# The second gate half asked for from the ScalarE queue, a slightly later x tile 1, and a fixed place for gelu on ScalarE, in a fused state-space and gated feed-forward kernel

## Chip, cores and metric

The kernel runs on one core of one Trainium2 chip. The metric is the device time of one execution in microseconds (us). The profile of an execution counts its "span" from the first recorded instruction; it is about 1.5 us shorter than the timed run. All runs in this text are in the fast state, except one run of d_before (188.62 us), which is marked slow. Ratios are the mean time of one kernel's fast runs over the mean of the other's fast runs of the same rounds, so they are not quite the ratios of the medians quoted beside them.

## The reference

The input x is 2048 rows of 512 columns in bf16. It is normalised row by row, and two branches read the result: a diagonal complex state-space scan, and a gated feed-forward layer of 1376 hidden columns. The output is their sum with x.

```python
xn = _layernorm(x)                                     # rows of 512
# branch A: h[t] = Lam_bar * h[t-1] + xn[t] @ B_bar.T ; y = 2 Re(h @ C.T) + xn * Dskip
# branch B:
ff = (gelu(xn @ w_gate) * (xn @ w_up)) @ w_down        # 512 -> 1376 -> 512
return x + y + ff
```

## The kernel before

x is cut into 16 tiles of 128 rows, four tiles to a block. TensorE (PE) multiplies, ScalarE (ACT) and VectorE (DVE) empty the PSUM banks and do the rest. The order of TensorE and of SyncE (SP, which issues most DMA) is the order of the program text. The order of ScalarE and VectorE is found by a list scheduler in Python, which works with estimated durations. `order_behind(a, b)` tells it to keep `a` behind `b` on the same engine.

The start of the kernel, with cuts marked:

```python
V(lambda e: e.memset(WRM.ap, 0.0), 150, [], [WRM], "wrm")             # zeros for the warm-up matmuls
half = V(lambda e: e.memset(HALF.ap, 0.5), D_TINY, [], [HALF], "half")
GATE["table"] = ACT(lambda e: e.activation(SCR.ap, HALF.ap[:, 0:1], ACTF.Gelu_apprx_tanh), 100, [HALF], [SCR], "gelu0")
# ... cut ...
ld_x0(0)                                                # x tile 0, 128 KB, SyncE queue
S.order_behind(ld_x0(1, "scalar"), GATE["table"])       # x tile 1, ScalarE queue
ld_wg0(0, "sync")                                       # first gate half: weight rows 0 to 255, 192 KB
ld_wg0(1, "sync")                                       # second gate half: rows 256 to 511
S.order_behind(ld_x0(2, "scalar"), GATE["table"])       # x tile 2
ld_w(WU, WUc, ins["B_w_up"], 0)                         # up weights, 384 KB
ld_x0(3)
# ... cut: the rest of the weights ...
nwarm = 7                                               # matmuls of zeros, before any data is there
# ... cut ...
fill(2)                                                 # two more small ones
cent_T(0, tb, "AA")                                     # transposes of centred tile 0, ScalarE copies them out
cent_T(1, [wb])
for r in range(2): GT_mm(0, r, ub[0, r], [0], (0, 1))   # first gate half, 4 matmuls in all
for r in range(2): GT_mm(0, r, ub[0, r], [0], (2, 3))   # second gate half, 4 matmuls
fill(4)                                                 # four fillers
# ... cut: tile 1's gate group (8), four groups of up weights (16), tile 2's transposes among them ...
```

Later, in the B stage, eight products of x and B for each block go through PSUM, ScalarE copies them out ("B copy"), and the feed-forward part of the next block follows with gelu:

```python
# BU(b): 8 groups of 4 matmuls, each followed by
ACT(lambda e, ...: e.activation(SSc[k3][s][c].ap, PS[bank][:, :], ACTF.Copy), d_act(512), [BANK[bank]], [SSc[k3][s][c]], "evBu")
# GU(b): for each 128 hidden columns
GATE["last_gelu"] = ACT(lambda e, ...: e.activation(GG[kk].ap[0:m, :], PS[bg][0:m, :], ACTF.Gelu_apprx_tanh), ..., "gelu", after=GATE["before_gelu"])
ACT(lambda e, ...: e.activation(UPB[kk].ap[0:m, :], PS[bu][0:m, :], ACTF.Copy), ..., "evU")
```

The kernel uses eight PSUM banks in turn and makes TensorE wait for a bank's copy before it writes the bank again (in x1_late below, 0.5 us for one copy).

Of the kernel before, what the change touches and what calls it, by code (L numbers as in the profile page):

```python
# [10 lines left out]
ACTF = mybir.ActivationFunctionType  # L11
# [350 lines left out]
def d_pe(n_list):  # L362
    return sum(n / 2.4 + 2.5 for n in n_list)
def d_dve_tt2x(n): return 100.0 + 0.52 * n
# [4 lines left out]
def d_act(n, ptr=0): return 190.0 + 0.833 * n + 90.0 * ptr  # L369
# [3 lines left out]
def build(nc, ins, out):  # L373
    with ExitStack() as es:
        E = es.enter_context
        S = Sched(nc, es)
# [3 lines left out]
        PS = [E(nc.psum_tensor("PS%d" % i, [128, 512], F32)) for i in range(8)]  # L380
# [45 lines left out]
        WRM = A.alloc("WRM", [128], BF16)  # L426
# [40 lines left out]
        SSc = [[[A.sub(SSs[k][s], "SS%d_%d_%d" % (k, s, c), c) for c in range(2)] for s in range(KP)] for k in range(3)]  # L467
# [3 lines left out]
        V = lambda fn, dur, r, w, tag="", after=(): S.op("vector", fn, dur, r, w, tag, after)  # L471
        ACT = lambda fn, dur, r, w, tag="", after=(): S.op("scalar", fn, dur, r, w, tag, after)
        POOL = lambda fn, dur, r, w, tag="", after=(): S.op("gpsimd", fn, dur, r, w, tag, after)
        PE = lambda fn, dur, r, w, tag="": S.op("tensor", fn, dur, r, w, tag)

        V(lambda e: e.memset(WRM.ap, 0.0), 150, [], [WRM], "wrm")
        GATE = {"before_gelu": [], "nh": 0}
        SCR = A.alloc("SCR", [1], F32)
        half = V(lambda e: e.memset(HALF.ap, 0.5), D_TINY, [], [HALF], "half")
        GATE["table"] = ACT(lambda e: e.activation(SCR.ap, HALF.ap[:, 0:1], ACTF.Gelu_apprx_tanh), 100, [HALF], [SCR], "gelu0")  # L480
        POOL(lambda e: e.iota(IOT.ap, [[1, 128]], base=0, channel_multiplier=-1), 300, [], [IOT], "iota")
        GATE["ident"] = V(lambda e: e.tensor_scalar(IDN.ap, IOT.ap, 0.0, None, ALU.is_equal), d_dve_ts4x(128), [IOT], [IDN], "ident")
# [9 lines left out]
        def ld_w(W, Wc, src, ci, queue="sync", after=()):  # L492
            f0, f1 = FCH[ci]
            return S.dma(lambda e: e.dma_start(W.ap[:, :, f0:f1], src[:, f0:f1].rearrange("(k p) f -> p k f", p=128)),
                         512 * (f1 - f0) * 2, writes=[Wc[ci]], tag="ld_w", queue=queue, after=after)

        def ld_x0(j, queue="sync", after=()):
            return S.dma(lambda e, j=j: e.dma_start(X[j].ap, x2[128 * j:128 * (j + 1), :]), 128 * 1024, writes=[X[j]], tag="ld_x0", queue=queue, after=after)  # L498
        WG0h = [Buf("WG0h%d" % n, "sbx", n / 2, (n + 1) / 2) for n in range(2)]

        def ld_wg0(n, queue, after=()):
            return S.dma(lambda e: e.dma_start(WG.ap[:, 2 * n:2 * n + 2, 0:384],  # L502
                                        ins["B_w_gate"][256 * n:256 * (n + 1), 0:384].rearrange("(k p) f -> p k f", p=128)),
                  192 * 1024, writes=[WG0h[n]], tag="ld_w", queue=queue, after=after)
        ld_x0(0)
        S.order_behind(ld_x0(1, "scalar"), GATE["table"])
        ld_wg0(0, "sync")
        ld_wg0(1, "sync")
        S.order_behind(ld_x0(2, "scalar"), GATE["table"])
        ld_w(WU, WUc, ins["B_w_up"], 0)  # L510
        ld_x0(3)
        for ci in (1, 2):
# [44 lines left out]
        def next_bank():  # L557
            b_ = rstate["n"] % 8
            rstate["n"] += 1
            return b_  # L560
# [165 lines left out]
        def BU(b):  # L726
            k3 = b % 3
            for c, s in ([(c, s) for c in range(2) for s in range(KP)] if b == 0 else [(c, s) for s in range(KP) for c in range(2)]):
                bank = next_bank()

                def f(e, bank=bank, c=c, s=s, b=b):
                    ins_ = None
                    for dk in range(KD):
                        ins_ = e.matmul(PS[bank][:, :], BBT[c][dk].ap[:, 128 * s:128 * (s + 1)], XNT[b].ap[:, dk, :],  # L734
                                        start=(dk == 0), stop=(dk == KD - 1))
                    return ins_
                PE(f, d_pe([512] * 4), [BBT[c][dk] for dk in range(KD)] + XTr(b), [BANK[bank]], "Bu%d" % b)
                ACT(lambda e, bank=bank, k3=k3, s=s, c=c: e.activation(SSc[k3][s][c].ap, PS[bank][:, :], ACTF.Copy),  # L738
                    d_act(512), [BANK[bank]], [SSc[k3][s][c]], "evBu")

        def span_of(buf, s0, s1):
# [70 lines left out]
        def GU(b, fts=None):  # L812
            k2 = b % 2
            fts = list(range(KF) if fts is None else fts)
            banks = {}

            def mm(ft, W, Wc, bank, c0, c1, rd):
                m = FROWS[ft]

                def f(e):  # L820
                    ins_ = None
                    for dk in range(KD):
                        ins_ = e.matmul(PS[bank][0:m, c0:c1], W.ap[:, dk, 128 * ft:128 * ft + m], XNT[b].ap[:, dk, c0:c1],  # L823
                                        start=(dk == 0), stop=(dk == KD - 1))
                    return ins_
                PE(f, d_pe([c1 - c0] * 4), [Wc[wchunk(ft)]] + rd, [BANK[bank]], "GU%d" % b)

            for ft in fts:
                m = FROWS[ft]
                if m < 128:  # L830
                    GU_rest(b)
                    continue
                banks[ft] = (next_bank(), next_bank())
                bg, bu = banks[ft]
                kk = (KF * b + ft) % 3
                for (W, Wc, bank) in zip((WG, WU), (WGc, WUc), banks[ft]):
                    mm(ft, W, Wc, bank, 0, 512, XTr(b))
                GATE["last_gelu"] = ACT(lambda e, bg=bg, kk=kk, m=m: e.activation(  # L838
                    GG[kk].ap[0:m, :], PS[bg][0:m, :], ACTF.Gelu_apprx_tanh),
                    d_act(512), [BANK[bg]], [GG[kk]], "gelu", after=GATE["before_gelu"])  # L840
                ACT(lambda e, bu=bu, kk=kk, m=m: e.activation(UPB[kk].ap[0:m, :], PS[bu][0:m, :], ACTF.Copy),  # L841
                    d_act(512), [BANK[bu]], [UPB[kk]], "evU")
                V(lambda e, kk=kk, m=m, ft=ft, k2=k2: e.tensor_tensor(  # L843
                    HTt[k2][ft].ap[0:m, :], GG[kk].ap[0:m, :], UPB[kk].ap[0:m, :], ALU.mult),
                  d_dve_tt2x(512), [GG[kk], UPB[kk]], [HTt[k2][ft]], "hmul")
# [144 lines left out]
        TR(1)  # L990
        SKIP(0)
        GU(0, [7, 8, 9, 10])
        GATE["before_gelu"] = [tables_act([GATE["last_gelu"]])]
        SKIP(1)
        BU(0)
        CHAIN(0, 2)
        H0_T()
        BU(1)
        coefs()
        CHAIN(1)  # L1000
# [3 lines left out]
        late_loads()  # L1004
        scale_C()
        GU(1, [0, 1, 2, 10, 3, 4, 5, 6, 7, 8, 9])
        BU(2)
        CHAIN(2)
        DN(0, True)
        LN(3); SKIP(3)  # L1010
        GU(2, [0, 1, 2, 10, 3, 4, 5, 6, 7]); TR(3); GU(2, [8, 9])
        BU(3)
        CHAIN(3)
# [9 lines left out]
def bass_parallel_sum__ssm_conv_s5__geglu_ffn__prompt_kernel(  # L1023
    nc: bass.Bass,
    A_x: bass.AP,
    A_Lambda_re: bass.AP,
    A_Lambda_im: bass.AP,
    A_B_re: bass.AP,
    A_B_im: bass.AP,
    A_C_re: bass.AP,  # L1030
    A_C_im: bass.AP,
    A_log_dt: bass.AP,
    A_Dskip: bass.AP,
    B_x: bass.AP,
    B_w_gate: bass.AP,
    B_w_up: bass.AP,
    B_w_down: bass.AP,
    out: bass.AP,
):
    ins = {  # L1040
        "A_x": A_x, "A_Lambda_re": A_Lambda_re, "A_Lambda_im": A_Lambda_im,
        "A_B_re": A_B_re, "A_B_im": A_B_im, "A_C_re": A_C_re, "A_C_im": A_C_im,
        "A_log_dt": A_log_dt, "A_Dskip": A_Dskip,
        "B_w_gate": B_w_gate, "B_w_up": B_w_up, "B_w_down": B_w_down,
    }
    build(nc, ins, out)
# [28 lines left out]
```

## Time and profile before

| kernel before | |
|---|---|
| timed, three runs at first | 178.21 us median (178.1 to 178.65) |
| timed, six runs when the change was measured | 178.3 us median (178.1 to 178.65) |
| span of the profile | 176.8 us |
| first gate matmul | 5.40 us |
| start of TensorE's unbroken run to the end | 5.98 us |

From the page of the profile: the span, the busy time of the engines (us, share of the span, instructions; PEld is TensorE's weight load), and the shares of the chain that ended last.

```profile
span 176.8 us, 2507 instructions
PE 173.0 (98%) x888; PEld 84.2 (48%) x888; DVE 160.9 (91%) x283; ACT 89.3 (51%) x169; POOL 10.1 (6%) x25
PE 95%; DMA 2%; SPq 0%; DVE 0%; issue 0%
```

The chain is followed back from the last instruction to whatever released each step. In order of time (start, length, what; L698 are the gate and up matmuls of block 0, L920 the fillers, L863 the last products), from its first DMA on:

```profile
1.66 4.27 DMA arena<-in_B_w_gate_dram
5.93 0.05 issue
5.98 0.50 PE PS L698 x4
6.48 0.22 PE PS L920 x4
6.71 0.99 PE PS L698 x12
...
141.37 32.91 PE PS L863 x171
```

The kernel starts on the second gate half, which lands 4.27 us after it is asked for; from there to the end there is nothing but TensorE. The list of waits of the weight loads (us in total, times, longest) has the same wait:

```profile
PEld PS L698 <- DMA arena<-in_B_w_gate_dram: 0.3, 1, 0.3
```

The timeline of TensorE's matmuls in that stretch (start, us from first start to last end, engine, line, shapes, count):

```profile
4.44 0.86 PE L673 MATMUL PS<-arena 128*128 128x128 bf16 x8
5.40 1.08 PE L698 MATMUL PS<-arena 128*128 128x192 bf16 x8
6.32 0.39 PE L920 MATMUL PS<-arena 128*128 128x128 bf16 x4
6.54 1.15 PE L698 MATMUL PS<-arena 128*128 128x192 bf16 x12
7.53 0.39 PE L673 MATMUL PS<-arena 128*128 128x128 bf16 x4
```

From the first gate matmul (5.40) to tile 2's transposes (7.53) are 2.13 us. The work in it is 20 matmuls of 192 columns, which in this trace step by 82.5 ns when TensorE is undisturbed, and 4 fillers that step by 56 ns: 20 x 0.0825 + 4 x 0.056 = 1.87 us. The rest, 0.26 us, is the wait. This stretch, "gate to tile 2", is the ruler.

### The profile page before, as it was taken

To read this page: it belongs to the slowest core of one execution; us is meant where nothing else is said; L and a number is where in the kernel's file an instruction comes from. 1 tells how busy PE (TensorE), PEld (TensorE's weight loads), DVE (VectorE), ACT (ScalarE), POOL (GpSimd) and SP (SyncE) were. 2 spreads that over 40 slices of the span, in tenths; PEclk is the share of its full clock that TensorE was granted. 3 is DMA by queue.
4 is the path that set the end of the run, shared out by engine and by line. 5 is a ranking of instruction groups with operands and counts; after the bars stand their busy time and mean duration, and the time that the engine had idled before them with its cause. 6 is when DMAs were issued, how large, how long until landed. Compare 5 with 4: busy or idle time off the path is not lost.

```text
span 176.8 us, 2507 instructions
## 1 busy us (share of the span) xinstructions
PE 173.0 (98%) x888; PEld 84.2 (48%) x888; DVE 160.9 (91%) x283; ACT 89.3 (51%) x169; POOL 10.1 (6%) x25
## 2 busy tenths in 40 slices
PE   7999999999999999999999999999999999999994
PEld 2854464444544444444644444444454444444453
DVE  5978999998999979979999999899999999999911
ACT  4475578999676898003676593000757680000000
POOL 3212040220000000300000000000000000000000
DMA  5997989675799000011034000100001000000321
GB/s 166 306 317 167 194 193 164 62 150 118 171 255 307 6 0 0 0 61 59 4 61 88 2 0 0 33 30 30 30 0 30 4 0 0 0 0 19 104 77 43
DMA packets 33396, 14.36 MB, mean 81 GB/s; under 512 B 23688, under 2 KB 33384, under 8 KB 33384
## 3 DMA queue, kind: packets, MB, share of 16 engines
q1 hardware_dynamic: 33072, 13.94, 34.7%
q10 hardware_dynamic: 312, 0.27, 0.4%
q8 instruction: 7, 0.11, 0.3%
q14 instruction: 5, 0.04, 0.1%
HBM read 6.46 MB, written 2.10 MB: 48 GB/s over the span
## 4 chain that ended last, share of the span: by engine, by line
PE 95%; DMA 2%; SPq 0%; DVE 0%; issue 0%
PE PS L863 37%; PE PS L823 32%; PE PS L734 16%; PE PS L698 7%; PE PS L797 3%; DMA arena<-in_B_w_gate_dram 2%; PE PS L673 0%; SPq L502 0%; SPq L498 0%; DVE arena L881 0%; PE PS L920 0%
## 5 line engine op out<-in xcount | busy, mean ns | idle before, releaser
L863 PE MATMUL PS<-arena 128*128 128x512 bf16 (+3 forms) x323 | 66.2, 366 | 0.0
L823 PE MATMUL PS<-arena 128*128 128x512 bf16 x264 | 58.1, 379 | 0.0
L863 PEld LDWEIGHTS PS<-arena 128*128 128x128 bf16 (+1 forms) x323 | 30.8, 98 | 35.2
L823 PEld LDWEIGHTS PS<-arena 128*128 128x128 bf16 x264 | 25.8, 98 | 30.4
L838 ACT ACTIVATE arena<-PS 128x512 bf16<-128x512 f32 x33 | 19.8, 600 | 37.6 <-PE PS L823 33.0
L767 DVE TENSOR_TENSOR_SCAN arena<-arena 128x512 bf16<-128x512 f32 x32 | 38.6, 1253 | 0.0
L734 PE MATMUL PS<-arena 128*128 128x512 bf16 x128 | 28.1, 379 | 0.0
L841 ACT ACTIVATE arena<-PS 128x512 bf16<-128x512 f32 x33 | 19.8, 599 | 4.9 <-PE PS L823 4.9
L734 PEld LDWEIGHTS PS<-arena 128*128 128x128 bf16 x128 | 12.5, 98 | 14.9 <-issue 0.2
L855 ACT ACTIVATE PS<-arena 128x512 f32<-128x512 bf16 (+2 forms) x17 | 9.4, 580 | 17.6 <-DVE arena L881 17.1
L738 ACT ACTIVATE arena<-PS 128x512 bf16<-128x512 f32 x32 | 17.4, 604 | 1.1 <-PE PS L734 1.1
L881 DVE TENSOR_TENSOR arena<-PS,arena 128x512 bf16<-128x512 f32 (+2 forms) x17 | 11.0, 654 | 7.3 <-PE PS L863 7.1
L843 DVE TENSOR_TENSOR arena<-arena 128x512 bf16<-128x512 bf16 x33 | 12.9, 415 | 1.0 <-ACT arena L841 0.9
L698 PE MATMUL PS<-arena 128*128 128x192 bf16 (+2 forms) x80 | 13.0, 315 | 0.2
L624 DVE BATCH_NORM_STATS2 arena<-arena 128x6 f32<-128x512 bf16 x16 | 10.2, 682 | 0.8 <-DMA arena<-in_A_x_dram 0.8
L756 DVE TENSOR_TENSOR arena<-arena 128x4096 bf16<-128x4096 bf16 (+1 forms) x5 | 9.2, 1860 | 0.4 <-ACT arena L620 0.4
L698 PEld LDWEIGHTS PS<-arena 128*128 128x128 bf16 x80 | 7.2, 98 | 5.0 <-DMA arena<-in_B_w_gate_dram 0.3
L754 DVE TENSOR_TENSOR arena<-arena 128x4096 bf16<-128x4096 bf16 (+1 forms) x5 | 9.2, 1859 | 0.0
L780 DVE TENSOR_TENSOR arena<-arena 128x4096 bf16<-128x4096 bf16 x4 | 9.1, 2284 | 0.0
L779 DVE TENSOR_TENSOR arena<-arena 128x4096 bf16<-128x4096 bf16 x4 | 9.1, 2283 | 0.0
L707 ACT ACTIVATE arena<-PS,arena 128x192 bf16<-128x192 f32 (+1 forms) x16 | 6.6, 448 | 3.0 <-PE PS L698 2.0
L710 DVE SCALAR_TENSOR_TENSOR arena<-PS,arena 128x192 bf16<-128x192 f32 (+1 forms) x16 | 6.6, 447 | 1.5 <-ACT arena L707 1.3
(84 smaller groups left out, 110.1 us busy)
## 6 DMA issues: line engine op xcount, KB each, us to landing
out_dram<-arena SPq DMA_DIRECT2D x15, 128.0 KB, 1.7
arena<-in_A_x_dram SPq DMA_DIRECT2D x3, 512.0 KB, 5.2
arena<-in_B_w_down_dram SPq DMA_DIRECT2D x1, 1280.0 KB, 7.3
arena<-in_B_w_gate_dram SPq DMA_DIRECT2D x2, 256.0 KB, 5.3
arena<-in_B_w_up_dram SPq DMA_DIRECT2D x2, 256.0 KB, 5.5
arena<-in_B_w_gate_dram SPq DMA_DIRECT2D x1, 480.0 KB, 5.8
arena<-in_B_w_up_dram SPq DMA_DIRECT2D x1, 480.0 KB, 5.9
arena<-arena SPq DMA_TRANSPOSE x25, 2.5
```

The source lines that it names most:

```text
L624: return (V(lambda e: e.bn_stats(ST[tt].ap, X[tt].ap), d_dve_1x(512), [X[tt]], [ST[tt]], "bnst"), V(lambda e: e.bn_aggr(MVt[b][j].ap, ST[t ...
L698: ins_ = e.matmul(dst, XCd(j, k), WGU[:, us[0]:us[-1] + 1, k, f0:f1], start=(k == 0), stop=(k == KD - 1))
L734: ins_ = e.matmul(PS[bank][:, :], BBT[c][dk].ap[:, 128 * s:128 * (s + 1)], XNT[b].ap[:, dk, :], start=(dk == 0), stop=(dk == KD - 1))
L738: ACT(lambda e, bank=bank, k3=k3, s=s, c=c: e.activation(SSc[k3][s][c].ap, PS[bank][:, :], ACTF.Copy), d_act(512), [BANK[bank]], [SSc[k3][ ...
L767: V(lambda e, g=g, rb=rb, init=init: e.tensor_tensor_scan(g.ap, rb, g.ap, init, ALU.mult, ALU.add), d_dve_scan(512), [g, PA[RRr]] + ([CARc ...
L823: ins_ = e.matmul(PS[bank][0:m, c0:c1], W.ap[:, dk, 128 * ft:128 * ft + m], XNT[b].ap[:, dk, c0:c1], start=(dk == 0), stop=(dk == KD - 1))
L838: GATE["last_gelu"] = ACT(lambda e, bg=bg, kk=kk, m=m: e.activation(GG[kk].ap[0:m, :], PS[bg][0:m, :], ACTF.Gelu_apprx_tanh), d_act(512), ...
L841: ACT(lambda e, bu=bu, kk=kk, m=m: e.activation(UPB[kk].ap[0:m, :], PS[bu][0:m, :], ACTF.Copy), d_act(512), [BANK[bu]], [UPB[kk]], "evU")
L843: V(lambda e, kk=kk, m=m, ft=ft, k2=k2: e.tensor_tensor(HTt[k2][ft].ap[0:m, :], GG[kk].ap[0:m, :], UPB[kk].ap[0:m, :], ALU.mult), d_dve_tt ...
L855: ACT(lambda e: e.activation(PS[bank][:, c0:c1], X[tt].ap[:, c0:c1], ACTF.Copy), d_act(c1 - c0), [X[tt]], [BANK[bank]], "seed")
L863: ins_ = e.matmul(PS[bank][:, c0:c1], l_[:, 128 * j:128 * (j + 1)], r_[:, c0:c1], start=False, stop=last and n == len(ops) - 1, skip_group ...
L881: V(lambda e: e.tensor_tensor(OUTB[ko].ap[:, c0:c1], PS[bank][:, c0:c1], XD[tt].ap[:, c0:c1], ALU.add), d_dve_1x(c1 - c0), [BANK[bank], XD ...
```

## The change

The intent is to have the second gate half there when TensorE wants it: it goes second in the ScalarE queue, where x tile 2 was; tile 2 goes third in SyncE's. Tile 1 is asked for a little later (it waits for the second memset), and gelu is tied behind the last B copy.

```diff
-        V(lambda e: e.memset(WRM.ap, 0.0), 150, [], [WRM], "wrm")
         half = V(lambda e: e.memset(HALF.ap, 0.5), D_TINY, [], [HALF], "half")
+        wrm = S.order_behind(V(lambda e: e.memset(WRM.ap, 0.0), 150, [], [WRM], "wrm"), half)
...
         ld_x0(0)
-        S.order_behind(ld_x0(1, "scalar"), GATE["table"])
+        S.order_behind(ld_x0(1, "scalar", [wrm]), GATE["table"])
         ld_wg0(0, "sync")
-        ld_wg0(1, "sync")
-        S.order_behind(ld_x0(2, "scalar"), GATE["table"])
+        S.order_behind(ld_wg0(1, "scalar", [wrm]), GATE["table"])
+        ld_x0(2)
...
-                ACT(lambda e, bank=bank, ...: e.activation(SSc[k3][s][c].ap, PS[bank][:, :], ACTF.Copy),
+                GATE["evBu"] = ACT(lambda e, bank=bank, ...: e.activation(SSc[k3][s][c].ap, PS[bank][:, :], ACTF.Copy),
...
                     d_act(512), [BANK[bg]], [GG[kk]], "gelu", after=GATE["before_gelu"])
+                S.order_behind(GATE["last_gelu"], GATE.pop("evBu", None))
```

More of the change, by code (lines that the diff above doesn't have):

```diff
@@ L737, in BU @@
                 PE(f, d_pe([512] * 4), [BBT[c][dk] for dk in range(KD)] + XTr(b), [BANK[bank]], "Bu%d" % b)
-                ACT(lambda e, bank=bank, k3=k3, s=s, c=c: e.activation(SSc[k3][s][c].ap, PS[bank][:, :], ACTF.Copy),
+                GATE["evBu"] = ACT(lambda e, bank=bank, k3=k3, s=s, c=c: e.activation(SSc[k3][s][c].ap, PS[bank][:, :], ACTF.Copy),
                     d_act(512), [BANK[bank]], [SSc[k3][s][c]], "evBu")
```

## The prediction

> **What bounds the kernel.** TensorE. In the chain of waits it holds 95% of the 176.8 us span, and from 5.98 to 174.29 us the chain is TensorE pieces alone, back to back. VectorE is busy 91%, ScalarE 51% (engine table), and the list of waits shows TensorE waiting for neither in the steady part. So two places can move the time: the first 6 us, and any new hole in TensorE's stream.
>
> The first 6 us, from the timelines of single engines: x tile 0 asked for at 0.74, its statistics at 3.08, transposes 4.44, first gate matmuls 5.40, needing only the first gate half. The weight loads then stand 0.31 us (to 5.97) for the second half, asked for at 1.66 as third load of the SyncE queue and landing 4.27 us later, at 5.93.
>
> **The change.** No arithmetic is added or removed; TensorE's instruction order is identical.
> 1. x tile 1 (ScalarE queue) waits for the second memset, which ends at 0.96: issued about 1.03 instead of 0.91. The two memsets already ran in the now fixed order.
> 2. The second gate half is second in the ScalarE queue: issued about 1.46 instead of 1.66, with 128 KB ahead of it in its queue instead of 320. [...] In this trace tile 2, in that place, landed about 4.7 us (issue near 1.35 plus about 3.4, from the issue table's median). With half as many bytes again I estimate 5.0 to 5.4.
> 3. x tile 2 is third in SyncE's queue, issued 1.66 instead of 1.35: landing perhaps 5.3 to 5.9. VectorE wants it at 5.58; TensorE wants its transposes about 7.2 (centred tile ready at 6.86 before): slack about 0.4 us.
> 4. ScalarE: the sine table load moves one B copy ahead; gelu is tied behind the last B copy. The copies ran several us ahead of the matmuls that reuse the banks, so nothing reaches TensorE. VectorE's order is shuffled; its last chain ended at 161.35 us, 1.2 us before the last state matmuls (about 162.5).
>
> **On the critical path.** At most the 0.31 us wait. Next limits: the second half of tile 0's copies, about 5.5; the first four matmuls, about 5.7. So the second gate group can start near 5.72: 0.25 us gained. A later tile 1 may bring tile 0 up to 0.1 us earlier. Against it: up weights landed about 6.97 and are wanted near 7.1, and a late tile 2. Net about 0.25 us, carried unchanged to the end.
>
> **Predicted: 177.95 us**, range 177.6 to 178.4. Faster by over 2%: 0.01; within 2%: 0.98; slower: 0.01.
>
> **What would show it.** Right: the weight loads' wait for the second gate half is gone or under 0.1 us; it lands near 5.2; the chain starts through x tile 0, its statistics and ScalarE's copies instead of a gate load; TensorE's unbroken run starts near 5.7 and ends near 174.0; span near 176.5. Wrong: the gate half lands no earlier than 5.7; VectorE waits for tile 2 past 6.0 and TensorE for its transposes; up weights become the new wait; TensorE holes around the B stage (25 to 40 us) or near 162 us.
>
> **What would make it wrong.** Sharing between queues that favours SyncE's, or tile 0 slowed by the competing gate half, would turn the gain into nothing or a 0.2 us loss. A late VectorE chain at 162 us would cost up to 1 us. The three runs of before spread by 0.55 us, more than the gain.

The landing at 5.0 to 5.4 is the estimate from tile 2's landing in the trace, and 178.21 us (the first three runs) less the 0.25 us of gain is about 177.95.

## The result, and the profile after

| | before | changed |
|---|---|---|
| timed, six runs each | 178.3 us median (178.1 to 178.65) | 178.33 us median (178.05 to 178.88) |
| ratio of fast runs | | 1.0003, 95% interval 0.9985 to 1.0021 |
| span of the profile | 176.8 | 176.6 |
| second gate half lands | 5.93 | 5.25 |
| first gate matmul | 5.40 | 5.25 |
| tile 2's transposes | 7.53 | 7.34 |

No gain shows in the timed runs, though the wait is gone. The page after:

```profile
span 176.6 us, 2492 instructions
PE 172.3 (98%) x873; PEld 84.5 (48%) x888; DVE 160.7 (91%) x283; ACT 89.5 (51%) x169; POOL 11.4 (6%) x25
PE 98%; issue 1%; DVE 0%
```

Fifteen matmul records are missing from this trace (873 of 888); the short "issue" pieces that its chain shows after 18 us are their places, and no engine or DMA is named there. The chain, with L914 the warm-up, L921 the fillers and L673 transposes (lines of the kernel have moved by one):

```profile
1.02 3.17 PE PS L914 x7
4.19 0.21 PE PS L921 x2
4.40 0.93 PE PS L673 x8
5.33 0.97 PE PS L698 x8
6.29 0.22 PE PS L921 x4
6.52 0.99 PE PS L698 x12
...
161.57 12.54 PE PS L864 x76
```

The DMA has left the chain; it now begins with TensorE's own warm-up. The complete list of waits of the weight loads has no gate half any more:

```profile
PEld PS L914 <- issue: 1.4, 5, 0.3
PEld PS L914 <- DVE arena L479: 1.0, 1, 1.0
PEld PS L921 <- issue: 0.6, 2, 0.3
PEld PS L698 <- issue: 0.2, 1, 0.2
PEld PS L673 <- DVE arena L933: 0.2, 1, 0.2
```

But look at the timeline of the same stretch:

```profile
4.29 1.03 PE L673 MATMUL PS<-arena 128*128 128x128 bf16 x8
5.25 1.04 PE L698 MATMUL PS<-arena 128*128 128x192 bf16 x8
6.13 0.39 PE L921 MATMUL PS<-arena 128*128 128x128 bf16 x4
6.35 1.15 PE L698 MATMUL PS<-arena 128*128 128x192 bf16 x12
7.34 0.39 PE L673 MATMUL PS<-arena 128*128 128x128 bf16 x4
```

Eight gate matmuls without a wait took 1.04 us, nearly the 1.08 us of before with its wait, while twelve of the same shape just after took 1.15. The ruler "gate to tile 2" reads 2.09 us, not 1.87. The starts of the single matmuls say why: the eight step by 112, 160, 160, 117 and then 82 ns. The transposes before them step by 107 ns here; in the profile of before the last two steps among them were 80 and 56 ns. **TensorE was at half speed until about 5.75 us in this execution, and until about 5.0 us in that of before.** The first four gate matmuls cost 0.22 us more, which is most of the wait that was removed.

One trap: the profile's own PEclk does not show this. The windows view of the changed kernel answers 1.00 for 0 to 5.5 us, a stretch at half speed, because the events of the clock that the trace keeps begin only with the change to full speed. That event itself agrees with the steps: the trace of the changed kernel has it at 5.74 us. (The views do not print it; it was read from the packed trace. Before and q_nofill have no such event; in the nine other profiles of the table below it lies within 0.1 us of the steps.)

### The profile page after: what moved, and what is told of

The parts are those of the page before. It is cut to its first block, busy times and chain, and to the rows that moved or that the text cites. A ratio compares the mean times of both kernels' runs of the same rounds, so it can differ in the third digit from the quotient of the medians.

```text
span 176.6 us, 2492 instructions
## 1 busy us (share of the span) xinstructions
PE 172.3 (98%) x873; PEld 84.5 (48%) x888; DVE 160.7 (91%) x283; ACT 89.5 (51%) x169; POOL 11.4 (6%) x25
## 4 chain that ended last, share of the span: by engine, by line
PE 98%; issue 1%; DVE 0%
PE PS L864 37%; PE PS L823 32%; PE PS L734 16%; PE PS L698 7%; PE PS L797 3%; PE PS L914 2%; PE PS L673 1%; PE PS L921 0%; DVE arena L882 0%; DVE arena L479 0%; DVE arena L478 0%
## 5 line engine op out<-in xcount | busy, mean ns | idle before, releaser
L823 PE MATMUL PS<-arena 128*128 128x512 bf16 x258 | 57.5, 379 | 0.3
L838 ACT ACTIVATE arena<-PS 128x512 bf16<-128x512 f32 x33 | 19.8, 601 | 37.5 <-PE PS L823 33.7
L734 PE MATMUL PS<-arena 128*128 128x512 bf16 x125 | 27.8, 379 | 0.2
L738 ACT ACTIVATE arena<-PS 128x512 bf16<-128x512 f32 x32 | 17.3, 602 | 1.3 <-PE PS L734 1.3
```

Of the source, the lines that this page charges most:

```text
L734: ins_ = e.matmul(PS[bank][:, :], BBT[c][dk].ap[:, 128 * s:128 * (s + 1)], XNT[b].ap[:, dk, :], start=(dk == 0), stop=(dk == KD - 1))
L738: GATE["evBu"] = ACT(lambda e, bank=bank, k3=k3, s=s, c=c: e.activation(SSc[k3][s][c].ap, PS[bank][:, :], ACTF.Copy), d_act(512), [BANK[ba ...
L823: ins_ = e.matmul(PS[bank][0:m, c0:c1], W.ap[:, dk, 128 * ft:128 * ft + m], XNT[b].ap[:, dk, c0:c1], start=(dk == 0), stop=(dk == KD - 1))
L838: GATE["last_gelu"] = ACT(lambda e, bg=bg, kk=kk, m=m: e.activation(GG[kk].ap[0:m, :], PS[bg][0:m, :], ACTF.Gelu_apprx_tanh), d_act(512), ...
```

## The experiments

The theories on the table:

- **A**: the wait is removed, but the gate matmuls now meet the half-speed warm-up of TensorE, whose end moves from execution to execution, gives part of the gain back and scatters the runs.
- **B**: the scatter comes from the landing of x tile 0.
- **C**: the new order of ScalarE or VectorE costs later what the start gains.
- **D** (formed later): the wait of before was an accident of one profile; landings vary.
- **E** (formed later): the delay of tile 1 disturbs the scheduler's order and the tie repairs it.

For A, the traces show two speeds of the same matmuls: in the two profiles above 107 and then 56 ns steps for 128 columns, and in the second also 160 and then 82 for 192. The change comes at a different moment in every profile: with the usual seven warm-up matmuls, which begin at 1.02 us, between 4.2 and 7.0 us (table "All starts together"), that is 3.2 to 6.0 us after the first of them; without them at 8.5 and 9.0. What sets the moment is not shown.

### a_again: the changed kernel, a second time

No edit.

> The changed kernel again, unaltered, for a second profile and five more rounds. In its first profile the wait for the second gate half was gone and the first gate matmul began at 5.25 instead of 5.40 us, but the first four gate matmuls stepped at 112 to 160 ns instead of 82, so the run after them began only 0.19 us earlier. Theory A: the step is TensorE's clock at half speed in its warm-up, whose end moves from run to run (about 5.0 us in the profile of before, 5.7 in that of the change). Then this profile will show a different moment of the change of speed, the span will follow it (each us of half speed after 5.25 costs about 0.5 us), and the timed runs will again spread by 0.5 us or more; ratio 0.997 to 1.001. Theory B, the spread is of the landings of x tile 0: then the first statistics move by as much as the span does. Theory C, the new order of ScalarE or VectorE costs something later: then holes of TensorE appear after 9 us and the ratio is 1.000 or more.

Measured: 178.76 us median (178.11 to 178.86, 6 runs), ratio 1.0001 (0.9983 to 1.0018). The span was 177.3 us. Its chain at the start:

```profile
5.36 1.36 PE PS L698 x8
6.72 0.42 PE PS L921 x4
```

The first gate matmul began at 5.29, as early as in the first profile (5.25). But the matmuls stepped by 160 ns, and the fillers by 106, until about 7.0 us. The ruler reads 2.68 us (5.29 to 7.97), 0.59 more than in the first profile of the same kernel, and the span is 0.63 longer. The first statistics began at 2.97 against 2.93, so tile 0's landing cannot be it (B falls for this pair). From tile 2's transposes to the start of the last matmul are 166.53 us, against 166.54 and, before the change, 166.51: nothing is lost later (C falls for the changed kernel).

### queue_only: the exchange of queues alone

```diff
-        ld_wg0(1, "sync")
-        S.order_behind(ld_x0(2, "scalar"), GATE["table"])
+        S.order_behind(ld_wg0(1, "scalar"), GATE["table"])
+        ld_x0(2)
```

The comparison of orders shows every compute engine unchanged.

> The kernel before with only the queues of the second gate half and of x tile 2 exchanged; every compute engine keeps the order of before. Theory A and every theory in which the queue is what matters: the wait of 0.31 us is gone here too, the gate half lands before 5.3 us, ratio as that of the whole change (0.997 to 1.001). If the delay of x tile 1 is needed for tile 0 to land earlier, statistics start at 3.05 to 3.10 us as before and not at 2.93.

Measured: 178.18 us median (178.1 to 178.42, 5 runs), ratio 0.998 (0.9967 to 0.9994). The gate half landed at 5.13 and was not waited for; full speed came at about 6.2 us, the ruler reads 2.29, the span is 176.9. Statistics began at 3.02. The first claim holds: the exchange alone removes the wait. Whether this kernel is truly 0.4 us faster than the full change, as the two ratios of these rounds (0.998 and 1.0001) suggest, stays open: five or six runs that scatter like these do not carry it, although its own interval lies below 1.

### d_before and d_after: all loads held back

Both kernels with three large memsets on VectorE ahead of all loads, and 26 warm-up matmuls (that of the changed kernel; its twin is edited alike, with tile 1 and 2 behind `d1`):

```diff
+        dly = [wrm]                       # three memsets of 128x4096 bf16, then three tiny ones: d0, d1, d2
...
-        ld_x0(0)
-        S.order_behind(ld_x0(1, "scalar", [wrm]), GATE["table"])
+        ld_x0(0, "sync", [d0])
+        S.order_behind(ld_x0(1, "scalar", [d2]), GATE["table"])
...
-        nwarm = 7
+        nwarm = 26
```

> The kernel before with all loads held back about 6.5 us by three large memsets on VectorE and with 26 instead of 7 warm-up matmuls, so that TensorE is at full clock long before the first gate matmul. Only to be compared with its twin of the change. Theory A: the timed runs lie within 0.25 us of each other (0.55 us or more without the delay), the gate half is still waited for by about 0.3 us. Theory B: the spread stays at 0.5 us or more.

> The changed kernel with the same delay and warm-up. Theory A: no wait for the gate half, all gate matmuls at 82 ns from the first, and the time is shorter than that of its twin by 0.25 to 0.45 us, clear of a spread under 0.25 us. Theory C (the change loses later what it gains at the start): the difference to the twin is under 0.1 us though the start shows 0.3 us gained.

Measured: 187.2 us median (185.62 to 188.62, 6 runs, of which 188.62 is slow and the five fast ones end at 188.02) and 186.18 us median (185.13 to 186.44, 5 runs). **The design failed**: the scatter grew instead of falling. The warm-up did reach full speed (its weight loads step by 427 ns until about 6.5 us in d_before and 5.7 in d_after, and by about 211 ns from then on). It was over at 9.0 to 9.5 us, tile 0's transposes came at 11.3, and after this gap d_after's trace has half speed again, from 12.69 to 16.11 us. The windows view of d_after shows it (window, length, busy us and counts, then the granted share of the clock, DMA share, GB/s):

```profile
8.00:14.00 6.00, 3.84 (x33) 2.85 (x32) 3.89 (x13) 1.87 (x5) 0.90 (x2) 0.89 0.89 256
14.00:20.00 6.00, 6.00 (x45) 4.54 (x44) 3.92 (x12) 3.14 (x8) 0.89 (x2) 0.82 1.29 324
```

In d_before's profile the clock stayed at 1.00 in both windows. The gap, as idle time of the weight loads before the transposes, was 2.14 us in d_after and 1.81 in d_before; that it was the gap which brought half speed back in d_after is not shown. The granted clock is on record for the timed runs too, and here it orders them: d_before's spans are 184.1 and 184.5 us at 0.999, 185.6 to 186.5 at 0.991 and 187.1 at 0.982; d_after's are 183.6 at 1.0 and 184.5 to 184.9 at 0.991. The pair says nothing about the wait; it does show that the runs at 0.991 are longer than those at 0.999 or 1.0 of the same kernel, by 1.1 to 2.4 us in d_before and 0.9 to 1.3 in d_after, the profiled run of d_after (184.9 us, 0.991) among them (where the clock fell in the other timed runs was not looked at). It also showed two things taken up below: d_before had no wait for the gate half, and it had a hole of 0.7 us in its weight loads near 51 us, at a B copy, which d_after had not.

### b_again: the kernel before, a second time

No edit.

> The kernel before, unaltered, for a second profile. So far the moment at which TensorE goes to full clock (about 5.0 us in the first profile of before, 5.75 and 7.0 in the two of the change, 6.2 in the exchange of queues alone) orders the spans: 176.6 at 5.75, 176.9 at 6.2, 177.3 at 7.0, half a us per us. Theory A: this profile follows the line of before: 176.8 if the moment is before 6.0, and 0.5 us more for each us after it, and the wait for the gate half shrinks to nothing when the first four gate matmuls run at half speed. Theory D: the wait for the gate half was an accident of one profile, landings vary by more than 0.5 us from run to run; then it is absent here also with a full clock at 5.4 us.

Measured: 178.74 us median (177.88 to 179.3, 4 runs), span 177.3. Its chain at the start:

```profile
5.49 1.36 PE PS L698 x8
6.86 0.32 PE PS L920 x4
```

The eight gate matmuls are the same 1.36 us as in a_again. Full speed came at about 6.9 us. The gate half landed at 5.06 and nobody waited for it. So the same late clock gives the kernel before and the changed kernel the same span: 177.3 both, with the last matmul starting at 174.51 and 174.50. A and D are both right in part: the clock scatters the runs, and the wait is not there in every execution of before.

### n_before and n_after: without the warm-up matmuls

```diff
-        PE(fwarm, d_pe([512] * nwarm) * 1.6, [WRM], [BANK[wb]], "warm")
```

> The kernel before without the seven warm-up matmuls, so that TensorE is surely at half speed for the first gate matmuls. Slower than before by 1 to 2.5 us. Theory A: no wait for the second gate half over 0.05 us is left, since four matmuls at 160 ns from 5.40 end after it has landed at 5.93.

> The changed kernel without the warm-up matmuls. Theory A: faster than its twin of before by no more than 0.2 us, from tile 0 landing earlier alone, as there is no wait left to remove. If the wait counts for its full 0.25 us whatever the clock: faster by 0.4 us.

Measured: 179.66 us median (179.39 to 180.17, 4 runs) and 179.56 us median (178.84 to 179.7, 4 runs), ratios to before 1.0064 and 1.0047. n_before was slower by about 1.1 us, as expected, but what both runs were to decide missed. In n_before the gate half landed only at 6.58 us, later than even half-speed matmuls want it (four steps of 160 ns from 5.56 end at 6.20), and was waited for:

```profile
PEld PS L698 <- DMA arena<-in_B_w_gate_dram: 0.6, 1, 0.6
```

The means differ by 0.31 us, between what the two theories asked for, so this pair does not decide. What it gives: the warm-up is worth about 1 us here, and a third landing of the gate half from the old queue.

### q_nofill: no fillers behind the gate groups

queue_only with one line less:

```diff
-        fill(4)
```

> The exchange of queues alone, and the four filler matmuls after the first two gate groups left out (0.22 us at full clock, 0.43 at half). They bridged the time in which TensorE had to wait; with the gate half there early they stand in its stream. Theory A: 0.15 to 0.4 us shorter than the exchange alone, ratio to before 0.996 to 0.998; a new wait of at most 0.1 us for tile 1's copies near 5.95 us or for the up weights. If the fillers were needed to keep the clock: slower.

Measured: 178.02 us median (177.74 to 178.19, 6 runs), ratio to before **0.9967 (0.9954 to 0.998)**, correct. This is the lowest mean, though the interval overlaps that of queue_only. The ruler reads 1.93 us without the fillers' 0.22, and a new wait stands in it, for the up weights, which landed at 6.84:

```profile
2.16 4.68 DMA arena<-in_B_w_up_dram
6.84 0.05 issue
6.89 0.51 PE PS L698 x4
```

Expected was at most 0.1 us for this; it was 0.3 us (0.24 in the steps of the matmuls). In this execution full speed came at about 5.05 us, so the fillers were not needed to get it. Since the kernel before was not run without fillers, this does not show that the gain depends on the queues.

### x1_late: tile 1 delayed, nothing else

```diff
-        V(lambda e: e.memset(WRM.ap, 0.0), 150, [], [WRM], "wrm")
+        wrm = S.order_behind(V(lambda e: e.memset(WRM.ap, 0.0), 150, [], [WRM], "wrm"), half)    # after half
-        S.order_behind(ld_x0(1, "scalar"), GATE["table"])
+        S.order_behind(ld_x0(1, "scalar", [wrm]), GATE["table"])
```

> The kernel before with only x tile 1 held back until the second memset (about 0.1 us later); the gate half and tile 2 stay in their old queues. So far tile 0's statistics began at 3.08, 3.10 and 3.24 us in three profiles with the old queues and at 2.87 to 3.02 in five with the new ones, two of which (3.02, 2.98) had no delay of tile 1. If the delay brings tile 0 in: under 3.03 here. If the exchange of queues does: 3.05 to 3.25. The wait for the gate half, 0.3 us, none, and 0.6 us with the old queues so far, may be there or not; the time within 0.2% of before.

Measured: 179.43 us median (178.69 to 179.65, 6 runs), ratio **1.0047 (1.0023 to 1.0071)**. A delay of 0.1 us for one load made the kernel 0.9 us slower in the mean (179.31 against 178.39). Both of TensorE's waits in it, beside the first memset, are new (engine, line, what it waited for; us in total, times, longest):

```profile
PE PS L698 <- DMA arena<-in_B_w_up_dram: 0.6, 1, 0.6
PE PS L797 <- ACT arena L738: 0.5, 1, 0.5
```

The first is the up weights, landing at 7.75. The second is a B copy (L738) for which the narrow matmuls (L797) near 45 us wait. Before, ScalarE did the last five B copies in a row, and after them it turned to gelu. From the timeline of before:

```profile
37.70 2.59 ACT L738 ACTIVATE arena<-PS 128x512 bf16<-128x512 f32 x5
```

In x1_late it did four, then three pairs of gelu (L838) and copy (L841), and only then the last B copy. Its timeline (in brackets the engine's idle time before, and what ended it):

```profile
38.33 2.08 ACT L738 ACTIVATE arena<-PS 128x512 bf16<-128x512 f32 x4
...
44.80 0.60 ACT L841 ACTIVATE arena<-PS 128x512 bf16<-128x512 f32 x1 [0.21 <-PE PS L823]
45.30 0.59 ACT L738 ACTIVATE arena<-PS 128x512 bf16<-128x512 f32 x1
45.94 0.33 ACT L804 ACTIVATE arena<-PS 128x192 bf16<-128x192 f32 x1
45.94 0.75 PE L797 MATMUL PS<-arena 128*128 128x192 bf16 x7 [0.52 <-ACT arena L738]
```

The bank of that copy is the one which TensorE wants next. From tile 2's transposes to the last matmul are 167.22 us instead of 166.51: 0.68 of the 0.71 are the longer step at this hole. The scheduler, working with estimates, had chosen another order of ScalarE because one load was estimated later. This is theory E. The hole accounts for 0.68 of the 0.9 us; the rest was not pinned down. Statistics began at 2.85.

### order_only: the tie alone

```diff
-                ACT(lambda e, bank=bank, ...: e.activation(SSc[k3][s][c].ap, ...
+                GATE["evBu"] = ACT(lambda e, bank=bank, ...: e.activation(SSc[k3][s][c].ap, ...
...
+                S.order_behind(GATE["last_gelu"], GATE.pop("evBu", None))
```

> The kernel before with only the tie of gelu behind the last B copy. In all eight undelayed profiles so far the time from the first transpose of tile 2 to the last matmul was 166.50 to 166.65 us, whatever ScalarE's and VectorE's order: so 166.5 here too, no hole of TensorE after 9 us, and the time within 0.2% of before. Theory C (the order costs something): over 166.7. Its start is that of before, a further look at the landing of the gate half in the old queue: theory D expects it to lie anywhere between 5.0 and 6.6 us.

Measured: 178.44 us median (177.93 to 178.67, 6 runs), ratio 0.9999 (0.9977 to 1.002); 166.51 us from tile 2's transposes to the last matmul, no hole. Every engine ran its instructions in the order of before, so the tie changed nothing here, and this counts as a third profile of before: where the order is already right, the tie is free. In this execution the *first* gate half landed at 5.36 and was waited for (0.4 us in the list of waits), the second at 5.76; statistics began at 2.73, the earliest of all.

### a_notie and x1_tie: with and without the tie

a_notie is the changed kernel without the three `evBu` edits; x1_tie is x1_late with them.

```diff
# a_notie, against the changed kernel (and the copy's handle is dropped)
-                S.order_behind(GATE["last_gelu"], GATE.pop("evBu", None))
# x1_tie, against x1_late (and the copy's handle is kept)
+                S.order_behind(GATE["last_gelu"], GATE.pop("evBu", None))
```

> The changed kernel without the tie of gelu behind the last B copy. The order of ScalarE alone shows that the last of the 16 B copies then runs after three pairs of gelu and copy instead of before them, as it did in the run that only delayed x tile 1; there TensorE stood 0.5 us at the first of the narrow matmuls near 45 us, for that copy. Theory E: the delay of tile 1 shifts the order that the scheduler finds, and the tie repairs it: hole of 0.4 to 0.6 us near 44 to 46 us, 166.9 to 167.1 us from the first transpose of tile 2 to the last matmul, all timed runs 0.5 us longer than those of the change (about 178.9 median). If the hole was of that one run: 166.5 and the time of the change.

> The delay of x tile 1 and the tie, without the exchange of queues. Theory E: no hole near 45 us, 166.5 us from tile 2's first transpose to the last matmul, the time 0.4 to 0.7 us below that of the delay alone and within 0.2% of before. The gate half, in the old queue, lands anywhere between 4.8 and 6.6 us; with the new queues it came at 5.13 to 5.50 in five profiles.

Measured: a_notie 178.83 us median (178.54 to 179.2, 6 runs), x1_tie 178.54 us median (178.23 to 178.72, 6 runs). a_notie has the hole, as its chain shows:

```profile
43.67 0.60 ACT arena L841
44.27 0.50 ACT arena L738
44.81 0.83 PE PS L797 x8
```

and 167.22 us from tile 2's transposes to the last matmul; x1_tie has no hole and 166.53. With the tie the delayed kernel went from 1.0047 to 0.9988 (0.9951 to 1.0025) of before, 0.8 us less in the mean, where the hole of the profile accounts for 0.68. E holds in both directions. The timed runs of a_notie (mean 178.87) are 0.4 us above those of the changed kernel (178.49 over its twelve runs, from other rounds); their ratio to before, 1.0012 (0.9971 to 1.0052), is wide, because one run of before in these rounds took 180.65. The size of the hole is read from the profile, not from these times.

The profile of a_notie happens to show the start with full speed from the very first transposes (56 ns steps at 4.29 us): first gate matmul 5.08, ruler 1.93 us, tile 2's transposes at 7.01, half a microsecond earlier than in the first profile of before. So the start can be that fast, when the clock is there. Then another limit appears: the first gate matmuls waited 0.19 us for ScalarE's copies.

### All starts together

Landings are from the traces; "full speed" is where the steps of the matmuls change. The last two columns are ruler and rest: first gate matmul to tile 2's transposes, and from there to the start of the last matmul. The work alone is 1.87 us (1.65 in q_nofill).

| profile | gate half lands | first gate matmul | full speed from | ruler | rest |
|---|---|---|---|---|---|
| *old queues* | | | | | |
| before | 5.93 | 5.40 | 5.0 | 2.13 | 166.51 |
| b_again | 5.06 | 5.42 | 6.9 | 2.58 | 166.51 |
| x1_late | 4.81 | 5.18 | 5.8 | 2.96 | 167.22 |
| order_only | 5.76 | 5.40 | 6.6 | 2.44 | 166.51 |
| x1_tie | 5.63 | 5.30 | 6.8 | 2.58 | 166.53 |
| n_before | 6.58 | 5.56 | 8.5 | 3.54 | 166.51 |
| *new queues* | | | | | |
| changed | 5.25 | 5.25 | 5.75 | 2.09 | 166.54 |
| a_again | 5.47 | 5.29 | 7.0 | 2.68 | 166.53 |
| queue_only | 5.13 | 5.34 | 6.2 | 2.29 | 166.50 |
| q_nofill | 5.16 | 5.30 | 5.05 | 1.93 | 166.50 |
| a_notie | 5.18 | 5.08 | 4.2 | 1.93 | 167.22 |
| n_after | 5.50 | 5.19 | 9.0 | 3.58 | 166.65 |

Three readings. The gate half lands between 4.81 and 6.58 us from the old place, and between 5.13 and 5.50 from the new one; with the new queues it was never waited for in six profiles, with the old ones it was in two of six. Leave out the profiles that waited for a DMA in the stretch (before, x1_late, q_nofill, n_before) and n_after, which has no warm-up: in the others the ruler grows with the moment of full speed, 1.93 at 4.2, 2.09 at 5.75, 2.29 at 6.2, 2.44 at 6.6, 2.58 at 6.8 and 6.9, 2.68 at 7.0. From 5.75 on that is about half a microsecond for each microsecond, with the old queues as with the new. And the rest is the same to within 0.04 us in the profiles without the hole, but for n_after, where half speed reached into tile 2's transposes.

## Why the prediction was right or wrong

The measured 178.33 us lie within the range of 177.6 to 178.4, close to its upper end, and "within 2%" was right. The point, 177.95, was not reached, and the range held the unchanged time, 178.3, too: that the number fell inside it does not confirm the gain. Nor do the runs exclude it: a gain of 0.25 us is a ratio of 0.9986, just inside both intervals of the changed kernel.

- **The bound** was right: TensorE's unbroken run, and only the start or a hole can move the time.
- **Issue and landing of the gate half** were right in kind: issued at 1.44, landed at 5.25 in the first profile (predicted 1.46, and 5.0 to 5.4), and the wait was gone. The estimate had a slip: it took 3.4 us from issue to landing for tile 2 in that queue, where the issue table has a median of 2.9 for the queue and the trace 3.24 for this load. The gate half landed before tile 2, third in SyncE's queue, in five of the six profiles with the new queues, but it had also been asked for earlier; so no run here shows how the queues share. The sign "the chain starts through x tile 0" did not come: the chain starts with TensorE's warm-up. The mean landing came 0.35 us earlier in the table (5.63 to 5.28), of which 0.2 to 0.3 us is the earlier issue (1.36 to 1.44 instead of 1.66); the larger effect was that the spread fell from 1.8 to 0.4 us. Why it fell was not isolated.
- **Tile 0 up to 0.1 us earlier through the delay of tile 1** was not shown. Its statistics began at 3.08 in the first profile and 2.93 after; but the earliest of all, 2.73, had no delay of tile 1. Sorted by that delay, the six profiles of the table with it have 2.85 to 2.98 (mean 2.91) and the six without 2.73 to 3.25 (mean 3.03): of the predicted size, but inside the scatter.
- **Tile 2** was harmless as predicted: landed at 5.51 and 5.83 in the two profiles of the change, VectorE began its statistics at 5.53 and 5.86, and TensorE waited for neither.
- **"Nothing reaches TensorE"** from ScalarE's new order was right for the changed kernel as a whole, but the reason given was too simple. In the profile of before the last B copy did end 3.7 us ahead of the narrow matmuls near 44 us (40.29 and 43.97). The delay of tile 1 alone opens a 0.68 us hole at a B copy, and the tie closes it. The tie was read as a detail; it is what makes the other edit harmless.
- **The step that failed** is the sum's main term: "So the second gate group can start near 5.72: 0.25 us gained", and "carried unchanged to the end". The first gate group was costed at full speed. In the first profile of the change it ran at half speed and the second group started at 5.80 (the wait had been replaced by 0.22 us of slow matmuls); in the second profile half speed cost 0.81 us (ruler 2.68 less 1.87). And the 0.31 us that were to be removed are not there in every execution of before. What is left in the mean is less than the twelve runs can show: ratios of 1.0003 and 1.0001, each with an interval of 0.18% either way, that is 0.3 us. What did start earlier was carried to the end but for 0.03 us, as the constant rest shows.
- **The scatter** was seen ("the three runs of before spread by 0.55 us, more than the gain") but its cause was not asked for. It was readable in the first profile: the steps of the transposes change from 107 to 56 ns right before the gate matmuls. That the clock is the largest single part of it is shown for the profiled executions (ruler 1.93 to 2.68 us in those with warm-up that waited for no DMA in it); for the other timed runs of these kernels it is inferred, since their recorded clock (0.999 or 1.0) does not show the half speed at the start.

## What to carry to other kernels

Before costing a wait in the first microseconds, look at the steps of TensorE's matmuls there: here 0.22 us of slow matmuls took the place of most of a 0.31 us wait, and full speed came between 4.2 and 7.0 us in ten profiles, so take several profiles of both kernels and compare a fixed point later on. Where a scheduler places instructions from estimates, an edit of 0.1 us at the start can reorder an engine 40 us later (here it opened a hole of 0.68 us near 45 us): compare the orders of every engine, and tie the pairs whose order matters, such as the copy that frees a bank and the work behind it.
